# Conversions of w_in beside attention on GpSimd, four early loads, and shared low parts of w_out

## The chip, the cores and the metric

The kernel runs on one core of one Trainium2 chip. The metric is device time of one execution in microseconds (us); lower is better. The engines are TensorE (PE in the rows, its weight loads PEld), VectorE (DVE), ScalarE (ACT), GpSimd (POOL) and SyncE (SP), which here only issues transfers. A name with a q behind it (SPq, POOLq) is an engine's queue of instructions that are not computation, such as transfers.

## The reference

Three parts follow one another. The inputs are float32 but for w_in and w_out, which are float64; the kernel reads these two as 64-bit words.

```python
# attention: q, k, v [4, 12, 448, 64]
scores = cap * np.tanh((q @ k.T / 8) / cap)
attn = softmax(scores)                     # sum + 1e-9
x = (attn @ v) -> [1792, 768]
# top-1 mixture of 8 experts, 768 -> 1024 -> 768
e = argmax(x @ w_gate); gate = softmax(x @ w_gate)[e]
x = gate * (relu(x @ w1[e]) @ w2[e])
# MLP, 768 -> 2048 -> 768
h = x @ w_in
g = (a0 + a1*h + a2*h**2 + a3*h**3) / (1 + |b0|*|h| + |b1|*h**2 + 1e-6)
out = g @ w_out
```

## The kernel before

One program runs the three parts. Within it the order in which each engine gets its instructions is the order in which the code issues them (`manual_schedule`), so where a line stands in the code decides what it waits behind. Each engine takes its instructions strictly in that order.

**Attention** runs over 24 pairs of heads (`attention`, n = 0 to 23; a batch is 6 pairs). A pair's scores go through tanh and exp on ScalarE in four chunks (L143 to L151), VectorE adds the chunks (`presum`, L157, two per pair, tile `ts`), and TensorE makes the products with v (L166, L168) and the sums S (L178). In the loop's order the sums of pair n-1 come in pair n, behind `presum(n - 1, 1)`. Two batches' gates and rows are worked in between. `between(n)` is called twice per pair with `more`, and each such call steps the generator `conv_in` once.

**Conversion of w_in** (`conv_in`) takes 48 such steps, three for each of 16 tiles n. A tile arrives as 128 x 1536 32-bit words (`ci_raw`, two buffers), the two halves of 768 float64 numbers. ScalarE makes the exponent part from the upper words (`conv_a0`, L1090, tile `ci_a`, one buffer) in step one, and the lower words' part (`conv_a1`, L1093, tile `ci_hl`) in step two. In step three VectorE shifts and merges (`conv_b`, L1096 and L1097), SP issues the load of tile n+2, and GpSimd adds (`conv_c`, L1100), rounds to the high part (`pcopy`, L259) and subtracts for the low part (L1145). SP stores the pair of parts to `wi` in the next tile's step two.

**The experts** run after the gate in slots of 128 tokens (`phase_b`, about 300 to 613 us), and convert w_out in the same manner beside them. Their weights' buffers are `w1h` and `w1l`, four each; at the end the MLP's rings are laid into these and other buffers that are free by then (`mlp_start`).

**The MLP** (`phase_c`, `blocks`) has 5 blocks of 3, 3, 3, 3 and 2 tiles of 128 tokens, with 16 steps (n) of 128 hidden units each. Step n does `first(n)` (18 matmuls with x and w_in, each a product of high and low parts, L1336 to L1338), `rational(n)` (five activations on ScalarE, L1348 to L1352, beginning with the Square; three operations on GpSimd, L1353 to L1355; reciprocal, product and low part of the result on VectorE, L1356 to L1362, with its rounding on ScalarE, L1361), and `second` for two earlier steps (L1371 to L1373): half nh = 0 of w_out with step n - 4 (`LAG`), half nh = 1 with step n - 16. The last 16 steps of the loop (n from 80) have no `first`: they are called the drain here, and the results are sent by GpSimd from the rows' order (L1382, L1383).

w_in's parts come back through `win_load` on GpSimd's queue (L1304) into a ring of four; loads 0 and 1 are issued in `mlp_start`, 2 and 3 in `phase_c`, and load n + 3 in step n. Parts of w_out come by SP as single float32 tiles and are split in place: `wout_high` rounds on ScalarE (L1316), `wout_low` subtracts (L1322), on VectorE for nh = 0 and on GpSimd for nh = 1. In the trace the buffers keep the names of their first use, so that `w1h` and `w1l`, `raw`, `ex` and `x` stand in the MLP for parts of these rings.

Of the kernel before, what the change touches and what calls it, by code (L numbers as in the profile page):

```python
# [8 lines left out]
F32 = mybir.dt.float32  # L9
F32R = mybir.dt.float32r  # L10
BF16 = mybir.dt.bfloat16
U32 = mybir.dt.uint32
I32 = mybir.dt.int32
AF = mybir.ActivationFunctionType
ALU = mybir.AluOpType
# [7 lines left out]
DM = H * D  # L23
# [17 lines left out]
class K:  # L41
# [1072 lines left out]
    def conv_in(self, pool):  # L1114

        w = self.i["w64"].bitcast(U32)
        raws = {}

        def load(n):
            if n < self.NF:  # L1120
                raws[n] = pool.tile([128, 2 * DM], U32, name=f"ci_raw{n}", tag="ci_raw", bufs=2)
                self.nc.sync.dma_start(out=raws[n], in_=w[n])

        def store(n):
            if n in done:
                self.nc.sync.dma_start(out=self.wi[n], in_=done.pop(n).bitcast(F32))

        done = {}
        load(0)
        load(1)  # L1130
        for n in range(self.NF):
            a = pool.tile([128, DM], U32, name=f"ci_a{n}", tag="ci_a", bufs=1)
            hl = pool.tile([128, 2 * DM], F32R, name=f"ci_hl{n}", tag="ci_hl", bufs=2)
            raw = raws.pop(n).rearrange("p (c w) -> p c w", w=2)
            r = hl[:, DM:].bitcast(U32)
            self.conv_a0(a, raw)
            yield
            self.conv_a1(r, raw)
            store(n - 1)
            yield  # L1140
            self.conv_b(a, raw)
            load(n + 2)
            self.conv_c(a, r)
            self.pcopy(hl[:, :DM], r.bitcast(F32))
            self.nc.gpsimd.tensor_tensor(out=hl[:, DM:], in0=r.bitcast(F32), in1=hl[:, :DM].bitcast(F32), op=ALU.subtract)  # L1145
            done[n] = hl
            yield
        store(self.NF - 1)
# [85 lines left out]
    def mlp_start(self):  # L1234
        raw = self.raw[0] + self.raw[1]
        h, l = self.w1
        W = 384
        cut = lambda tiles: self.ring(tiles, W)[1]
        self.rings = {"win": [-1, [h[2], l[2]]]}
        c = cut([h[3], l[3]])  # L1240
        wout = [(c[2 * k], c[2 * k + 1]) for k in range(4)]
        self.rings |= {"wos0": [0, wout[:2]], "wos1": [0, wout[2:]]}
        a, b, c, d = (cut([t]) for t in raw[1:5])
        self.rings |= {"wor0": [0, c[:3]], "wor1": [0, d[:3]], "u": [0, [*a[2:], b[0]]], "o": [0, [*b[1:], c[3], d[3], *cut(self.xg[:1])]]}
        c = cut(raw[5:8])
        self.rings |= {k: [0, c[3 * i : 3 * i + 3]] for i, k in enumerate("stpq")}
        for f in range(2):
            self.win_load(f)
        for f in range(3):
            self.wout_load(0, f)  # L1250
        xt = self.p_xt.rearrange("p a b -> p (a b)")
        self.rings["ph"] = [0, self.p_l1]
        self.rings["xt"] = [0, [self.p_ht[0], xt[:, :512]]]
        self.acc = [[xt[:, :512], xt[:, 512:], self.p_ht[0]], [self.p_ht[1], *self.p_l2]]
        h, l = (cut(t[:2]) for t in (h, l))
        self.x2 = [[h[:6], l[:6]], [h[6:], l[6:]]]

    def phase_c(self):
        W = 384
        with self.tc.tile_pool(name="mlp", bufs=1) as mp:  # L1260
            xh, xl = (self.ring([t.rearrange("p a b -> p (a b)")], W)[1] for t in (self.xh, self.xl))
            for k in range(2):
                self.rings[f"wos{k}"][1].append((xh[k], xl[k]))
            self.rings["win"][1] += [mp.tile([128, 2 * DM], F32R, name=f"win{k}") for k in range(2)]
            self.win_load(2)
            self.win_load(3)
            for t, nm in zip(self.x2[1], "hl"):
                t += [mp.tile([128, W], F32R, name=f"x2{nm}{k}") for k in range(2, 6)]
            self.gh, self.gl = ([mp.tile([128, W], F32R, name=f"g{p}{f}") for f in range(self.NF)] for p in "hl")
            self.blocks()  # L1270
# [48 lines left out]
    def wout_low(self, nh, n):  # L1319
        if 0 <= n < len(self.BLOCKS) * self.NF:  # L1320
            h, l, r = self.wout[nh, n]
            (self.nc.gpsimd if nh else self.nc.vector).tensor_tensor(out=l, in0=r, in1=h.bitcast(F32), op=ALU.subtract)  # L1322
            self.wout_load(nh, n + 3)

    def first(self, n, kcs=range(6), ph=None):
# [154 lines left out]
```

## Time and profile before

| | |
|---|---|
| time, median of 3 runs | 1146.98 us (1144.69 to 1149.13) |
| profiled execution | 1150.3 us; span 1148.7 us; mean granted clock 0.975 |
| PE busy, share of the span | 1059.4 us (92%) |
| DVE, ACT, POOL busy | 698.1 (61%), 695.4 (61%), 650.9 us (57%) |
| memory | 247.12 MB moved, mean 215 GB/s |

The span is the part of the execution between its first and last instruction in the profile. A row of a timeline gives the start, the time it took, the engine, line and operation, the tile written and read, and in square brackets the engine's idle time ahead of it and what ended that. The granted clock is TensorE's, 1.0 for its upper level of 2.4 GHz; a stretch at 0.5 runs at the lower, 1.2 GHz.

### The profile page before, as it was taken

Reading aid. Unit: us, or ns where it says so; the run is one execution under the profiler, and the core shown is the slowest. Engines: PE = TensorE matmul, PEld = TensorE weight load, DVE = VectorE, ACT = ScalarE, POOL = GpSimd, SP = SyncE. Lnnn points to the kernel's source line nnn. Section 1 sums busy time; section 2 is a strip of 40 time slices with the busy share of each in tenths; the row PEclk is TensorE's granted clock in tenths of the full one; section 3 lists DMA queues with packets and bytes.
Section 4 is the critical chain, followed back from the end, with each engine's and each line's share of the span. In section 5 each row is a group of like instructions: output and inputs, shape, how many; then the busy total and the mean of one; then the engine's idle time right before and its main releaser. Section 6 shows DMA issues by size and latency. Waiting matters only on the chain. (4 is left out here: it accounts for less than half of the span.)

```text
span 1148.7 us, 17160 instructions
## 1 busy us (share of the span) xinstructions
PE 1059.4 (92%) x5808; PEld 857.9 (75%) x5808; DVE 698.1 (61%) x857; ACT 695.4 (61%) x1084; POOL 650.9 (57%) x631
## 2 busy tenths in 40 slices
PE   6999999895899989998999689999999999999985
PEld 2232322234798888988988678999999999999984
DVE  2557575768839463856373677766666666665660
ACT  5978788672347452835362566666666666676552
POOL 2433333356426443554332656786788688779975
PEclk9999999997999999998999899999999999999998
DMA  6696968745598775797514556665677576657843
GB/s 168 210 268 191 265 203 249 231 174 193 191 361 323 275 264 202 279 327 261 205 61 148 198 171 194 221 207 184 200 234 220 174 223 210 205 185 235 252 147 96
DMA packets 96439, 247.12 MB, mean 215 GB/s; under 512 B 12320, under 2 KB 61376, under 8 KB 96320
## 3 DMA queue, kind: packets, MB, share of 16 engines
q1 hardware_dynamic: 78624, 161.22, 43.0%
q0 software_dynamic: 17248, 82.62, 22.4%
q10 hardware_dynamic: 448, 1.80, 0.4%
q8 instruction: 60, 0.98, 0.3%
q14 instruction: 59, 0.48, 0.1%
HBM read 202.93 MB, written 42.67 MB: 214 GB/s over the span
## 5 line engine op out<-in xcount | busy, mean ns | idle before, releaser
L1356 DVE RECIPROCAL raw<-raw 128x384 f32<-128x384 f32 (+1 forms) x80 | 191.3, 2392 | 163.0 <-POOL raw L1354 163.0
L834 PE MATMUL p_l<-w1h,x 128*128 128x512 f32 x432 | 144.0, 400 | 1.4 <-ACT x L798 1.4
L1353 POOL TENSOR_TENSOR ex<-ex 128x384 f32<-128x384 f32 (+1 forms) x80 | 79.3, 991 | 98.8 <-ACT ex L1350 98.1
L1348 ACT ACTIVATE ex<-p_l 128x384 f32<-128x384 f32 (+1 forms) x80 | 37.7, 471 | 145.7 <-PE p_l L1338 141.1
L1100 POOL TENSOR_TENSOR ci_hl<-ci_hl,ci_a 128x768 int32<-128x768 int32 x16 | 37.2, 2327 | 149.5 <-ACT ex L151 36.4
L855 PE MATMUL p_l<-w2h,hh 128*128 128x384 f32 x288 | 102.3, 355 | 10.2 <-issue 7.2
L136 PE MATMUL sc<-qq,kk 64*128 64x448 f32 (+1 forms) x384 | 96.5, 594 | 10.2 <-ACT ex L143 5.1
L857 PE MATMUL p_l<-w2h,hl 128*128 128x384 f32 x288 | 99.1, 344 | 2.3 <-DVE hl L800 2.3
L856 PE MATMUL p_l<-w2l,hh 128*128 128x384 f32 x288 | 98.8, 343 | 1.5 <-issue 1.5
L834 PEld LDWEIGHTS p_l<-w1h,x 128*128 128x128 f32 x432 | 82.0, 190 | 18.5 <-ACT x L798 2.2
L800 DVE TENSOR_TENSOR hl<-p_ht,hh 128x512 fp32r<-128x512 f32 x36 | 24.8, 690 | 106.3 <-ACT hh L798 106.1
L834 PE MATMUL p_l<-w1l,x 128*128 128x512 f32 x216 | 85.2, 396 | 0.9 <-POOL w1l L800 0.9
L1354 POOL TENSOR_TENSOR raw<-raw,ex 128x384 f32<-128x384 f32 (+1 forms) x80 | 79.8, 998 | 8.4 <-ACT raw L1352 1.2
L143 ACT ACTIVATE ex<-sc,icap 128x896 f32<-128x896 f32 x72 | 71.1, 1004 | 21.8 <-PE sc L136 21.4
L837 ACT ACTIVATE hr<-p_l 128x512 f32<-128x512 f32 x36 | 21.6, 599 | 103.2 <-PE p_l L834 103.2
L151 ACT ACTIVATE ex<-ex,cap 128x1792 f32<-128x1792 f32 (+1 forms) x48 | 76.9, 1603 | 1.0
L136 PEld LDWEIGHTS sc<-qq,kk 64*128 64x128 f32 (+1 forms) x384 | 29.9, 178 | 63.2 <-issue 32.9
L867 POOL DMA_DIRECT2D x2d<-y x36 | 20.5, 569 | 96.5 <-DVE y L860 63.5
L166 PE MATMUL av<-ex,vv 128*64 128x448 f32 x288 | 68.3, 562 | 4.0 <-ACT ex L151 4.0
L1336 PE MATMUL p_l<-w1h,win 128*128 128x384 f32 (+1 forms) x176 | 58.7, 334 | 11.3 <-DMA win<-wi 6.3
L1100 POOL TENSOR_TENSOR c_r<-c_r,c_a 128x768 int32<-128x768 int32 x20 | 36.9, 1845 | 49.2 <-ACT c_a L1090 34.3
L855 PEld LDWEIGHTS p_l<-w2h,hh 128*128 128x128 f32 x288 | 55.7, 193 | 11.3 <-issue 10.0
(341 smaller groups left out, 3302.6 us busy)
## 6 DMA issues: line engine op xcount, KB each, us to landing
win<-wi POOLq DMA_DIRECT2D x40, 768.0 KB, 4.6
raw<-in_w SPq DMA_DIRECT2D x34, 768.0 KB
ex<-in_w SPq DMA_DIRECT2D x32, 768.0 KB
raw<-wd SPq DMA_DIRECT2D x80, 192.0 KB
w1h<-wi POOLq DMA_DIRECT2D x20, 768.0 KB, 4.7
w1l<-wi POOLq DMA_DIRECT2D x20, 768.0 KB, 6.2
ex<-wd SPq DMA_DIRECT2D x80, 192.0 KB
ci_raw<-in_w SPq DMA_DIRECT2D x16, 768.0 KB
```

The lines of the kernel that those rows point to most:

```text
L136: nc.tensor.matmul(o, kk[half[a], 128 * c : min(128 * c + 128, S)], qq[half[a]], start=True, stop=True)
L143: nc.scalar.activation(out=es[n][:, 2 * c : 2 * c + 2], in_=pt[:, :, :S], func=AF.Tanh, scale=self.icap)
L151: nc.scalar.activation(out=e, in_=e, func=AF.Exp, scale=self.cap)
L166: nc.tensor.matmul(at[half[a], :S], vv[:, a, c], e[:, 2 * c + a], start=c == 0, stop=False, skip_group_check=True)
L834: nc.tensor.matmul(pt, a[:, kc, :], b, start=kc == 0 and k == 0, stop=kc == 5 and k == 2)
L855: nc.tensor.matmul(pt[:, :384], hh, wh, start=f == 0, stop=False)
L856: nc.tensor.matmul(pt[:, :384], hh, wl, start=False, stop=False)
L857: nc.tensor.matmul(pt[:, :384], hl, wh, start=False, stop=f == 7)
L1100: self.nc.gpsimd.tensor_tensor(out=r.bitcast(I32), in0=r.bitcast(I32), in1=a.bitcast(I32), op=ALU.add)
L1353: nc.gpsimd.tensor_tensor(out=q, in0=q, in1=s, op=ALU.mult)
L1354: nc.gpsimd.tensor_tensor(out=u, in0=u, in1=t, op=ALU.add)
L1356: nc.vector.reciprocal(out=u, in_=u)
```

## The change

It has three parts. In `conv_in` the two activations become `tensor_scalar` operations on GpSimd, in the first of a tile's three steps, together with the store of the tile before; `conv_b` and the load of tile n+2 come in the second and the rest in the third; `ci_a` has two buffers. In `mlp_start` the ring of `win` is laid into the last expert's four weight buffers and all four loads are issued there, and the ring for w_out's split gets new tiles in their place. In `wout_low` the engine depends on the step: for nh = 0 odd steps below 12 go to GpSimd, and for nh = 1 even steps from 66 on go to VectorE.

```diff
--- before.py
+++ after.py
@@ -1128,21 +1128,22 @@
         done = {}
         load(0)
         load(1)
+        P = self.nc.gpsimd
         for n in range(self.NF):
-            a = pool.tile([128, DM], U32, name=f"ci_a{n}", tag="ci_a", bufs=1)
+            a = pool.tile([128, DM], U32, name=f"ci_a{n}", tag="ci_a", bufs=2)
             hl = pool.tile([128, 2 * DM], F32R, name=f"ci_hl{n}", tag="ci_hl", bufs=2)
             raw = raws.pop(n).rearrange("p (c w) -> p c w", w=2)
             r = hl[:, DM:].bitcast(U32)
-            self.conv_a0(a, raw)
-            yield
-            self.conv_a1(r, raw)
+            P.tensor_scalar(out=a.bitcast(F32), in0=raw[:, :, 1].bitcast(F32), scalar1=2.0**-112, scalar2=0.0, op0=ALU.mult, op1=ALU.add)
+            P.tensor_scalar(out=r.bitcast(I32), in0=raw[:, :, 0], scalar1=2.0**-29, scalar2=0.0, op0=ALU.mult, op1=ALU.add)
             store(n - 1)
             yield
             self.conv_b(a, raw)
             load(n + 2)
+            yield
             self.conv_c(a, r)
             self.pcopy(hl[:, :DM], r.bitcast(F32))
-            self.nc.gpsimd.tensor_tensor(out=hl[:, DM:], in0=r.bitcast(F32), in1=hl[:, :DM].bitcast(F32), op=ALU.subtract)
+            P.tensor_tensor(out=hl[:, DM:], in0=r.bitcast(F32), in1=hl[:, :DM].bitcast(F32), op=ALU.subtract)
             done[n] = hl
             yield
         store(self.NF - 1)
@@ -1236,15 +1237,12 @@
         h, l = self.w1
         W = 384
         cut = lambda tiles: self.ring(tiles, W)[1]
-        self.rings = {"win": [-1, [h[2], l[2]]]}
-        c = cut([h[3], l[3]])
-        wout = [(c[2 * k], c[2 * k + 1]) for k in range(4)]
-        self.rings |= {"wos0": [0, wout[:2]], "wos1": [0, wout[2:]]}
+        self.rings = {"win": [-1, [h[2], l[2], h[3], l[3]]]}
         a, b, c, d = (cut([t]) for t in raw[1:5])
         self.rings |= {"wor0": [0, c[:3]], "wor1": [0, d[:3]], "u": [0, [*a[2:], b[0]]], "o": [0, [*b[1:], c[3], d[3], *cut(self.xg[:1])]]}
         c = cut(raw[5:8])
         self.rings |= {k: [0, c[3 * i : 3 * i + 3]] for i, k in enumerate("stpq")}
-        for f in range(2):
+        for f in range(4):
             self.win_load(f)
         for f in range(3):
             self.wout_load(0, f)
@@ -1260,10 +1258,8 @@
         with self.tc.tile_pool(name="mlp", bufs=1) as mp:
             xh, xl = (self.ring([t.rearrange("p a b -> p (a b)")], W)[1] for t in (self.xh, self.xl))
             for k in range(2):
-                self.rings[f"wos{k}"][1].append((xh[k], xl[k]))
-            self.rings["win"][1] += [mp.tile([128, 2 * DM], F32R, name=f"win{k}") for k in range(2)]
-            self.win_load(2)
-            self.win_load(3)
+                new = [tuple(mp.tile([128, W], F32R, name=f"wo{p}{k}{i}") for p in "hl") for i in range(2)]
+                self.rings[f"wos{k}"] = [0, [(xh[k], xl[k]), *new]]
             for t, nm in zip(self.x2[1], "hl"):
                 t += [mp.tile([128, W], F32R, name=f"x2{nm}{k}") for k in range(2, 6)]
             self.gh, self.gl = ([mp.tile([128, W], F32R, name=f"g{p}{f}") for f in range(self.NF)] for p in "hl")
@@ -1319,7 +1315,9 @@
     def wout_low(self, nh, n):
         if 0 <= n < len(self.BLOCKS) * self.NF:
             h, l, r = self.wout[nh, n]
-            (self.nc.gpsimd if nh else self.nc.vector).tensor_tensor(out=l, in0=r, in1=h.bitcast(F32), op=ALU.subtract)
+
+            eng = n % 2 if not nh and n < self.NF - self.LAG or nh and n >= (len(self.BLOCKS) - 1) * self.NF + 2 else nh
+            (self.nc.gpsimd if eng else self.nc.vector).tensor_tensor(out=l, in0=r, in1=h.bitcast(F32), op=ALU.subtract)
             self.wout_load(nh, n + 3)
 
     def first(self, n, kcs=range(6), ph=None):
```

The conversion of tile 0 in VectorE's order, in attention's second pair (`ex_127` are the exponentials of pair 0, `av` the products, `u` their copy). Before:

```order
L157 TENSOR_TENSOR ts_207<-ex_127 128x896
L157 TENSOR_TENSOR ts_207<-ts_207,ex_127 128x896
L182 COPY u_241<-av_209 128x448
L1096 TENSOR_SCALAR ci_a_200<-ci_a_200 128x768
L1097 SCALAR_TENSOR_TENSOR ci_a_200<-ci_raw_196,ci_a_200 128x768
L157 TENSOR_TENSOR ts_259<-ex_128 128x896
```

and now:

```order
L157 TENSOR_TENSOR ts_208<-ex_127 128x896
L1096 TENSOR_SCALAR ci_a_200<-ci_a_200 128x768
L1097 SCALAR_TENSOR_TENSOR ci_a_200<-ci_raw_196,ci_a_200 128x768
L157 TENSOR_TENSOR ts_208<-ts_208,ex_127 128x896
L182 COPY u_245<-av_210 128x448
```

The two rows of `conv_b` moved ahead of pair 0's second presum.

GpSimd's order at the end of the experts and the start of the MLP (`x2d` are the experts' results, `wi` the parts of w_in, the three TENSOR_TENSOR rows `rational`). Before:

```order
L1304 DMA w1h_1907<-wi 128x1536
L1304 DMA w1l_1910<-wi 128x1536
...
L1353 TENSOR_TENSOR ex_128<-ex_128 128x384
L1354 TENSOR_TENSOR raw_130<-raw_130,ex_127 128x384
L1355 TENSOR_TENSOR ex_127<-ex_127,ex_128 128x384
L1304 DMA win_9268<-wi 128x1536
L1304 DMA win_9269<-wi 128x1536
L1304 DMA w1h_1907<-wi 128x1536
```

and now (the lines moved up by four):

```order
L1300 DMA w1h_1907<-wi 128x1536
L1300 DMA w1l_1910<-wi 128x1536
L1300 DMA w1h_1968<-wi 128x1536
L1300 DMA w1l_1969<-wi 128x1536
...
L1351 TENSOR_TENSOR ex_128<-ex_128 128x384
L1352 TENSOR_TENSOR raw_130<-raw_130,ex_127 128x384
L1353 TENSOR_TENSOR ex_127<-ex_127,ex_128 128x384
L1300 DMA w1h_1907<-wi 128x1536
```

Two loads moved from behind the first `rational` to right behind the first two.

VectorE's last instructions, in the drain (`wol`, `x` and `w1h` are w_out's low parts). Before:

```order
L1358 TENSOR_TENSOR ex_127<-ex_128,raw_131 128x256
L1322 TENSOR_TENSOR w1h_1968<-raw_132,w1h_1968 128x384
L1362 TENSOR_TENSOR gl_9311<-ex_127,gh_9295 128x256
L1322 TENSOR_TENSOR w1h_1968<-raw_132,w1h_1968 128x384
L1322 TENSOR_TENSOR x_1904<-raw_132,x_1903 128x384
L1377 COPY raw_131<-p_l_2042 128x384
```

and now:

```order
L1356 TENSOR_TENSOR ex_127<-ex_128,raw_131 128x256
L1320 TENSOR_TENSOR x_1904<-raw_132,x_1903 128x384
L1360 TENSOR_TENSOR gl_9317<-ex_127,gh_9301 128x256
L1320 TENSOR_TENSOR wol_9271<-raw_132,woh_9270 128x384
L1320 TENSOR_TENSOR wol_9275<-ex_127,woh_9274 128x384
L1320 TENSOR_TENSOR wol_9273<-raw_132,woh_9272 128x384
L1320 TENSOR_TENSOR x_1904<-ex_127,x_1903 128x384
L1320 TENSOR_TENSOR wol_9277<-ex_127,woh_9276 128x384
L1320 TENSOR_TENSOR wol_9275<-ex_127,woh_9274 128x384
L1320 TENSOR_TENSOR x_1904<-ex_127,x_1903 128x384
L1320 TENSOR_TENSOR wol_9277<-ex_127,woh_9276 128x384
L1320 TENSOR_TENSOR wol_9275<-ex_127,woh_9274 128x384
```

Seven subtractions from `ex_127`, half nh = 1, came over from GpSimd.

## Rows read from the trace of the kernel before

**Rows 1.** Stretches: start:end, length, busy us (count) per engine, clock, DMA share, GB/s

```profile
0.00:30.00 30.00, 18.90 (x70) 6.58 (x70) 6.96 (x23) 15.78 (x16) 8.42 (x18) 0.94 0.66 177
30.00:90.00 60.00, 57.71 (x289) 17.10 (x290) 34.78 (x47) 50.92 (x51) 23.10 (x13) 1.00 0.79 231
632.00:670.00 38.00, 26.09 (x119) 25.14 (x118) 28.22 (x22) 19.03 (x38) 22.60 (x25) 0.82 0.59 198
800.00:1100.00 300.00, 296.67 (x1800) 295.69 (x1799) 197.33 (x214) 197.18 (x428) 241.08 (x283) 1.00 0.68 213
1114.00:1118.00 4.00, 3.84 (x13) 3.84 (x14) 1.47 (x4) 1.08 (x4) 3.53 (x4) 0.57 0.46 139
```

**Rows 2.** ACT's timeline, start of attention

```profile
17.01 0.89 ACT L1090 ACTIVATE ci_a<-ci_raw 128x768 f32<-128x768 f32 x1 [5.03 <-DMA ci_raw<-in_w]
```

**Rows 3.** PE's timeline, attention

```profile
18.85 3.43 PE L136 MATMUL sc<-qq,kk 64*128 64x448 f32 x8 [5.10 <-ACT ex L143]
...
24.03 0.57 PE L178 MATMUL S<-ts,sel 128*32 128x448 f32 x2
...
31.23 0.97 PE L166 MATMUL av<-ex,vv 128*64 128x448 f32 x4 [1.04 <-ACT ex L151]
...
89.70 0.57 PE L178 MATMUL S<-ts,sel 128*32 128x448 f32 x2 [0.62 <-DVE ts L157]
```

**Rows 4.** Source line L1090: duration min/median/max in ns, and what ended idle time

```profile
L1090 ACT ACTIVATE ci_a<-ci_raw x16: 879/916/940, 17.0 to 235.9; 128x768 f32<-128x768 f32 x16
...
  POOL ci_hl L1100: 5.7, 4
```

**Rows 5.** POOL's timeline, start of the MLP

```profile
633.81 1.13 POOL L1304 DMA_DIRECT2D win<-wi  x2
```

**Rows 6.** The page's DMA issues: count, KB each, median us to landing

```profile
win<-wi POOLq DMA_DIRECT2D x40, 768.0 KB, 4.6
```

**Rows 7.** PE's timeline, start of the MLP

```profile
638.51 0.66 PE L1336 MATMUL p_l<-w1h,win 128*128 128x384 f32 x1 [6.27 <-DMA win<-wi]
...
664.46 0.69 PE L1336 MATMUL p_l<-w1h,win 128*128 128x384 f32 x1 [2.41 <-DVE w1l L800]
```

**Rows 8.** PE's timeline, drain

```profile
1114.16 0.44 PE L1372 MATMUL p_xt<-w1h,gh 128*128 128x384 f32 x1 [1.85 <-DVE w1h L1322]
```

**Rows 9.** Waits, 1096 to 1149 us: total, times, longest

```profile
PE p_ht L1372 <- POOL w1l L1322: 3.0, 4, 1.1
```

**Rows 10.** Source line L259 (`pcopy`), as in rows 4

```profile
L259 POOL TENSOR_SCALAR ci_hl<-ci_hl x16: 830/834/1552, 29.0 to 250.4; 128x768 fp32r<-128x768 f32 x16
```

**Rows 11.** POOL's timeline, attention's second batch

```profile
93.48 1.82 POOL L1100 TENSOR_TENSOR ci_hl<-ci_hl,ci_a 128x768 int32<-128x768 int32 x1 [5.77 <-ACT ex L145]
```

**Rows 12.** DVE's timeline, attention

```profile
21.44 1.09 DVE L157 TENSOR_TENSOR ts<-ts,ex 128x896 f32<-128x896 f32 x1 [8.34 <-ACT ex L151]
...
24.69 0.55 DVE L1096 TENSOR_SCALAR ci_a<-ci_a 128x768 uint32<-128x768 uint32 x1
25.27 0.96 DVE L1097 SCALAR_TENSOR_TENSOR ci_a<-ci_raw,ci_a 128x768 uint32<-128x768 uint32 x1
...
94.19 1.14 DVE L518 TENSOR_SCALAR ji<-ri 112x4 int32<-112x4 int32 x1
95.36 0.16 DVE L520 TENSOR_TENSOR jt<-ri,ji 112x4 f32<-112x4 int32 x1
```

**Rows 13.** SP's queue, start

```profile
12.80 0.47 SPq L122 DMA_DIRECT2D kk<-in_k  x1
```

**Rows 14.** ACT's timeline, start of the MLP (Square of steps 1 and 2)

```profile
632.28 0.49 ACT L1348 ACTIVATE ex<-p_l 128x384 f32<-128x384 f32 x1 [0.44 <-PE p_l L1338]
...
644.21 0.49 ACT L1348 ACTIVATE ex<-p_l 128x384 f32<-128x384 f32 x1 [6.30 <-PE p_l L1338]
```

**Rows 15.** DVE's timeline, start of the MLP

```profile
658.43 1.37 DVE L1322 TENSOR_TENSOR x<-raw,x 128x384 fp32r<-128x384 f32 x1
```

**Rows 16.** POOL's timeline, drain

```profile
1127.71 1.00 POOL L1322 TENSOR_TENSOR w1l<-ex,w1l 128x384 fp32r<-128x384 f32 x1
```

## The prediction

> **What bounds the kernel now.** I read the table of stretches first, to see where an engine is full. From 800 to 1100 us, inside the MLP's blocks, TensorE is busy 296.67 of 300 us, and at attention's full pace, 30 to 90 us, 57.71 of 60 [rows 1]: in both only the last per cents can be won. Three stretches are thinner: the first 30 us with 18.90 busy; the head of the MLP, 632 to 670 us, with 26.09 of 38 us at a mean granted clock of 0.82; and the drain, where after a pause 13 matmuls take 3.84 us at a clock of 0.57, against 1800 in 300 us, 0.167 each, in the full blocks [rows 1]. So the change is priced in four places, and the timelines of the engines tell what TensorE waits for in each.
>
> In the start, ScalarE stands 5.03 us until 17.01 for the first raw tile, because the conversion L1090 is in its queue; TensorE's scores follow at 18.85 after 5.10 us of nothing, and the sums S at 24.03 [rows 2, 3]. Later ScalarE waits 4 times, 5.7 us in all, for GpSimd's L1100 to free the one buffer `ci_a` [rows 4]; behind the first of these TensorE loses 1.04 at 31.23, behind the second 0.62 before the sums at 89.70 [rows 3].
>
> In the MLP head TensorE waits 6.27 us for `win`, until 638.51: the load went out on GpSimd at 633.81 only, and one takes 4.6 us to land [rows 5 to 7]. In the drain it waits for the subtractions of w_out's split: 1.85 us for VectorE's at 1114.16, then 3.0 us in four waits for GpSimd's [rows 8, 9].
>
> **Part 1, conversions on GpSimd.** Off ScalarE go 32 activations at about 0.91, 29 us: the 16 of L1090 by their median of 0.916, the 16 of L1093 taken alike [rows 4]. GpSimd gets 32 operations with one tensor input of 128x768. The trace of before has none of just this form. The nearest is `pcopy`, the same engine, operation and size with another stride and output type: median 0.834 [rows 10]. The upper end is 1.82, L1100 with two inputs [rows 11], the lower `pcopy`'s shortest, 0.83. I take 0.85, close to `pcopy`: 27 us, at the upper end 58. GpSimd is busy 23.10 of 60 us there [rows 1], so there is room for it.
>
> Start: ScalarE no longer stands at 11.98. But VectorE now has `conv_b` of tile 0 ahead of the second presum, and that needs the raw tile (17.01) and one GpSimd operation (0.85). It runs from about 17.9 for 0.55 + 0.96, then the presum for 1.1, to 20.5, where it ended at 22.5 before [rows 12]. The sums, which then wait for nothing else, would start near 20.6, 3.4 us before 24.03. TensorE idles longer ahead of them and may lose clock, so I take **2.5**, ends 1 and 5. The wait at 31.23 goes: **1.0**. The three like it at a batch's start lie between 0.62 and 1.04; 0.8 each: **2.4**.
>
> Against this stands VectorE. While GpSimd's L1100 ran from 93.48 to 95.30, the tiny `ji` took 1.14 and ended with it; `jt`, right after, took 0.16 [rows 11, 12]. So a VectorE operation can be held for the rest of a GpSimd operation, up to 0.85 for each of 32 new ones, 27 us in all. Most of it is hidden, since VectorE works 34.78 of 60 us [rows 1] and TensorE asks for its result later; I count 0.4 in sum. Attention: 2.5 + 1.0 + 2.4 - 0.4 = **5.5**, ends -2 and 10.
>
> The Trainium skill has a rule that speaks against this part ("SBUF — State Buffer", section "Who interferes with whom"): VectorE and GpSimd share one port pair, which whoever issues first holds alone for its whole instruction, while ScalarE has ports of its own. The trace agrees with it (1.14 against 0.16). Taken at its word for every overlap it gives the fourth rival; with most holds hidden it leaves the sum as it is.
>
> On SP the load of raw tile 2 now stands ahead of pair 3's q, k and v and waits for `conv_b` of tile 0. They went out at 12.80 [rows 13] and will go at about 20; pair 3's scores come behind 31.23, so 10 us remain, and nothing is lost. The stores of `wi` move one step; they are read after 613 us.
>
> **Part 2, four loads at once, w_out's low parts of block 0 shared.** Loads 2 and 3 move from behind rational(0), at 633.81, to right behind loads 0 and 1, at about 616. If the four landed strictly one after the other at 4.6 us [rows 6], the third would be there at about 616 + 3 x 4.6 = 630 and the fourth at 634.5. first(2) can start at 638.51 - 6.27 = 632.24 [rows 7], and first(3) needs its own 18 matmuls of 0.167 later [rows 1], at 635.2. Covered; the pause goes, and the half clock behind it.
>
> What is late next is the chain behind it. ScalarE's Square of step 2 started at 644.21 after 6.30 of waiting [rows 14]; it can start when `gh` of step 0 and the high split before it are through, at about 637.9: 6.3 gained. From there on VectorE and GpSimd set the pace. VectorE's low part of step 1, 1.37, stood ahead of a reciprocal [rows 15]; it is now GpSimd's, at 1.00 [rows 16]. TensorE's next pause, 2.41 until 664.46 [rows 7], shrinks, and the slow matmuls behind it, worth about 1. GpSimd was busy 22.60 of 38 us [rows 1] and its rational can stand up to 1.0 behind a new low part; I take 1.2 back in all. 6.3 + 1.4 + 1.0 - 1.2 = **7.5**. The lower end is 3, if VectorE and GpSimd hold each other as they did the 1.37; the upper 10, both pauses and the 1.37. The blocks behind run at TensorE's pace and pass the shift on whole.
>
> **Part 3, drain.** Of the 1.85 at 1114.16 I take half, 0.9: VectorE's low part there stands behind its own reciprocal and product, and half of the parts change engine. The 13 slow matmuls cost 3.84 - 13 x 0.167 = 1.7 over full speed [rows 1]; after the shorter pause at 31.23 the products ran at full pace [rows 3], so I count 1.0 of it. Then GpSimd did each low part in 1.00 between sends [rows 16] while VectorE was idle; sharing takes 2 of the 3.0 us of waits [rows 9]. 3.9, so **4**; ends 1 (the transfers of w_out bind instead) and 6.5 (all of it).
>
> **Sum.** 5.5 + 7.5 + 4 = 17. The profiled execution took 1150.3 (span 1148.7), so 1133.3 by its count; it lies 3.3 over the median of the runs shown, 1146.98, and from that the forecast is **1130.0**. A measurement of this kernel can tell about 0.5%, 5.7 us, from no change.
>
> **Rivals.**
> 1. *Attention gives nothing.* Holds of VectorE and the wait for the first raw tile, only moved to VectorE, eat the 5.5. For it: `ji` at 1.14. Against: TensorE's waits on ScalarE are seen and their cause is removed. 11.5 gained: 1135.5.
> 2. *The head trades one wait for another.* VectorE, 28.22 of 38 us busy [rows 1], keeps the pace; 3 of 7.5, so 12.5 gained: 1134.5.
> 3. *All at its upper values.* ScalarE was the fuller helper in attention, 50.92 of 60 us [rows 1]; without 29 us of conversions most pauses close, 10, with 9 in the head and 6 in the drain: 1122.
> 4. *Slower.* The new operations cost 1.82 like two-input ones [rows 11] and hold VectorE's presums, on which TensorE's sums wait: 58 us of holds, half of them reaching TensorE, 29, less the 11.5 of the other parts and the 4.4 of ScalarE's waits: 1160. It decides from 16 us of reached holds on, 9 of 32 at 1.82 or 19 at 0.85. Against it: GpSimd already works 23.10 of 60 us there, most of it two-input, and TensorE idles 2.3 [rows 1].
> 5. *The early loads don't act.* They collide with the last expert's transfers and land no sooner than needed: the head gives 0: 1137.5. The bound of one after the other speaks against it.
>
> **Chances.** Forecast 0.55, the rivals in turn 0.14, 0.10, 0.12, 0.05, 0.04. The forecast's own spread, from the ends of its terms, is about 7 to either side. The range is **1118 to 1142**: it holds the forecast and the single rivals but the fourth, and leaves out the sum of several lower ends, and of all upper ends. Faster by over 0.5% (under 1141.2) is all but the fourth rival and the worst of the first, second and fifth together, 0.89; within 0.5% 0.06; slower 0.05.
>
> **What would show it.** Right: no wait of ScalarE for the raw tile and the first sums at 20 to 22; the moved operations at 0.8 to 0.95 on GpSimd; first(2) right behind first(1) and step 2's Square 6 us sooner against it; a granted clock over 0.9 in the head; in the drain low parts on both engines in turn, and less than 1.5 us of waits for GpSimd's. Wrong: moved operations over 1.3 us; TensorE's waits for VectorE in attention growing by more than those for ScalarE shrink; a `win` wait still ahead of first(2), or its Square less than 4 us sooner.

## The result and the profile after

The changed kernel takes 1126.80 us (median of 4 runs, 1125.03 to 1128.83), the kernel before, run beside it, 1146.35. The ratio is 0.9828, interval 0.9800 to 0.9855: 19.6 us less. The forecast was 1130.0, 17 us less than before, with a range of 1118 to 1142.

The profiled execution of the change took 1125.84 us (span 1124.0), 24.5 less than that of before. It is more than the medians differ. From the first to the last relu of the experts, code that the change doesn't touch, the profiled executions of all the kernels below spread from 348.5 to 352.8 us; before took 352.4 there and the change 349.7. So 2.7 of the 24.5 lie in a stage that varies by as much on its own. Another 1.4 lie between the Squares of steps 16 and 79 of the MLP, where each execution takes either about 379.9 or about 381.4, whichever parts of the change it has. Stages are therefore compared below over several runs.

The table of stretches of the changed kernel, at the places of [rows 1] (head and drain moved with the program):

```profile
0.00:30.00 30.00, 21.66 (x78) 6.77 (x78) 10.20 (x24) 16.70 (x16) 14.77 (x22) 0.94 0.77 211
30.00:90.00 60.00, 59.68 (x302) 17.87 (x302) 37.24 (x52) 45.21 (x43) 33.19 (x21) 1.00 0.77 235
622.34:660.34 38.00, 30.17 (x162) 28.84 (x161) 31.86 (x26) 25.58 (x51) 30.80 (x32) 0.96 0.60 187
790.00:1090.00 300.00, 297.98 (x1818) 297.29 (x1818) 192.56 (x217) 201.34 (x440) 242.22 (x286) 1.00 0.67 212
1092.00:1096.00 4.00, 3.38 (x19) 3.39 (x20) 3.77 (x7) 1.75 (x4) 3.61 (x4) 1.00 0.48 150
```

TensorE's share rose where it was thin: the head from 26.09 to 30.17 us of 38, at a clock of 0.96 for 0.82; the drain's start now does 19 matmuls in 4 us at full clock, 13 before. The 60 us of attention went from 57.71 to 59.68, and the full blocks are as they were. What TensorE still waits for, in its timeline:

```profile
20.80 0.57 PE L178 MATMUL S<-ts,sel 128*32 128x448 f32 x2 [3.00 <-DVE ts L157]
...
96.09 0.57 PE L178 MATMUL S<-ts,sel 128*32 128x448 f32 x2 [1.78 <-DVE ts L157]
...
214.91 0.57 PE L178 MATMUL S<-ts,sel 128*32 128x448 f32 x2 [2.94 <-DVE ts L157]
...
631.16 0.44 PE L1334 MATMUL p_l<-w1h,w1h 128*128 128x384 f32 x1 [2.33 <-ACT ex L1349]
...
638.78 0.44 PE L1370 MATMUL p_xt<-wol,gh 128*128 128x384 f32 x1 [4.04 <-DVE wol L1320]
...
1092.62 0.44 PE L1370 MATMUL p_xt<-x,gh 128*128 128x384 f32 x1 [1.06 <-DVE x L1320]
```

The sums of pair 0 start at 20.80 (24.03 in [rows 3]), behind a new wait of 3.00 for VectorE. Behind that wait TensorE is slow for a while: from 22 to 25 us its granted clock is 0.51 in the change and 0.95 in before, as the two windows show, the change first:

```profile
22.00:25.00 3.00, 3.00 (x10) 0.46 (x8) 1.37 (x1) 1.06 (x2) 2.83 (x3) 0.51 1.02 309
```

```profile
22.00:25.00 3.00, 3.00 (x18) 0.65 (x16) 1.39 (x3) 2.96 (x3) 0.00 (x0) 0.95 0.00 0
```

The 5.10 before the scores of [rows 3] and the 6.27 for `win` of [rows 7] are gone; the 1.85 of [rows 8] is 1.06. The moved operations by source line, and `pcopy` beside them:

```profile
L1137 POOL TENSOR_SCALAR ci_a<-ci_raw x16: 875/912/1807, 16.7 to 228.1; 128x768 f32<-128x768 f32 x16
...
L259 POOL TENSOR_SCALAR ci_hl<-ci_hl x16: 832/1552/1823, 22.5 to 238.6; 128x768 fp32r<-128x768 f32 x16
```

The moved operations take 0.91 in the median, as the activations did [rows 4], but `pcopy`, 0.834 in [rows 10], now takes 1.55.

From the timelines I read five numbers for each kernel: ScalarE's first copy of the sums (L264, "start"), the three distances from one batch's first such copy to the next batch's (the third holds pair 20), the Square of step 16 of the MLP less that of step 1 ("head"), and the last matmul's end less the Square of step 79 ("drain").

| kernel | start | three batches | head | drain |
|---|---|---|---|---|
| before | 49.83 | 58.78, 58.80, 63.93 | 93.87 | 32.29 |
| the change | 47.09 | 59.50, 57.91, 59.90 | 84.18 | 28.39 |
| e1, conversion alone | 48.93 | 59.50, 57.90, 59.89 | 91.69 | 32.50 |
| e2, loads alone | 50.52 | 58.78, 58.79, 64.59 | 85.96 | 32.30 |
| e3, low parts of block 1 alone | 50.64 | 58.78, 58.79, 63.90 | 91.09 | 30.70 |
| e4, drain alone | 50.55 | 58.79, 58.78, 63.91 | 92.98 | 27.63 |
| e5, change on ScalarE | 50.37 | 57.78, 57.79, 59.18 | 84.16 | 28.52 |
| e6, change, merge late | 42.38 | 60.53, 60.43, 66.28 | 84.15 | 28.28 |
| e7, change, doubled operations | 49.55 | 57.90, 57.90, 63.27 | 84.11 | 27.98 |
| e8, change, tile 0 late | 42.80 | 57.90, 57.89, 59.89 | 84.67 | 27.85 |
| e9, e8 with ScalarE | 42.43 | 57.78, 57.79, 59.18 | 84.07 | 27.81 |
| e10, before, second buffer | 49.25 | 58.41, 58.40, 63.73 | 93.02 | 32.48 |
| e11, e5 with one buffer | 48.77 | 57.79, 57.78, 59.18 | 84.20 | 27.60 |
| e12, e8 with an early low part | 43.56 | 57.89, 57.91, 61.28 | 85.46 | 27.80 |

Each row is one execution. Start, head and drain scatter by 1 to 2 us for the same code. The batches repeat to 0.1 with three exceptions, all of the clock: the 59.50 of the change and e1 against the 57.90 of e7, e8 and e12, the 61.28 of e12 against e8's 59.89, and e2's 64.59 (its granted clock is 0.54 from 223 to 226 us, 0.72 from 222 to 225 in before). The same pause of TensorE, 1.78 before the sums, is followed by a lower granted clock in the change and by a full one in e8, as windows on the two show, the change first:

```profile
95.00:100.00 5.00, 3.91 (x14) 0.82 (x14) 4.83 (x10) 1.57 (x2) 1.72 (x2) 0.72 0.58 210
```

```profile
90.00:95.00 5.00, 3.22 (x20) 0.89 (x20) 4.86 (x10) 2.52 (x3) 2.43 (x2) 1.00 0.59 210
95.00:100.00 5.00, 5.00 (x27) 1.48 (x26) 2.62 (x4) 2.71 (x3) 4.08 (x3) 1.00 0.65 197
```

The clock's fall there costs 1.6 us, and whether it comes differs between executions.

### The profile page after: what moved, and what is told of

Its sections match the earlier page's. It is cut to its first block, busy times and chain, and to the rows that moved or that the text cites. A ratio compares the mean times of both kernels' runs of the same rounds, so it can differ in the third digit from the quotient of the medians.

```text
span 1124.0 us, 17161 instructions
## 1 busy us (share of the span) xinstructions
PE 1053.4 (94%) x5808; PEld 851.6 (76%) x5808; DVE 698.7 (62%) x858; ACT 671.9 (60%) x1052; POOL 690.2 (61%) x662
## 5 line engine op out<-in xcount | busy, mean ns | idle before, releaser
L136 PE MATMUL sc<-qq,kk 64*128 64x448 f32 (+1 forms) x384 | 98.0, 603 | 5.2 <-DMA kk<-in_k 5.2
L1100 POOL TENSOR_TENSOR ci_hl<-ci_hl,ci_a 128x768 int32<-128x768 int32 x16 | 32.5, 2033 | 88.3 <-DVE ci_a L1097 68.6
L136 PEld LDWEIGHTS sc<-qq,kk 64*128 64x128 f32 (+1 forms) x384 | 29.6, 178 | 58.2 <-issue 40.0
L1100 POOL TENSOR_TENSOR c_r<-c_r,c_a 128x768 int32<-128x768 int32 x20 | 36.9, 1845 | 48.0 <-ACT c_a L1090 32.4
L1334 PE MATMUL p_l<-w1h,w1h 128*128 128x384 f32 (+1 forms) x176 | 57.0, 324 | 6.1 <-DVE x2l L800 2.6
```

What stands on the lines that cost most here:

```text
L136: nc.tensor.matmul(o, kk[half[a], 128 * c : min(128 * c + 128, S)], qq[half[a]], start=True, stop=True)
L1100: self.nc.gpsimd.tensor_tensor(out=r.bitcast(I32), in0=r.bitcast(I32), in1=a.bitcast(I32), op=ALU.add)
```

## The experiments

### The four parts alone (e1 to e4)

e1 is the kernel before with the diff of `conv_in` alone, e2 with that of `mlp_start` and `phase_c`, e3 and e4 with one half of the rule in `wout_low`:

```diff
 # e3
+            eng = n % 2 if not nh and n < self.NF - self.LAG else nh
 # e4
+            eng = n % 2 if nh and n >= (len(self.BLOCKS) - 1) * self.NF + 2 else nh
```

> Only the conversion beside attention is changed (GpSimd, new order of its three steps, two buffers of ci_a). If its saving is local and stays, the copy of the first sums (L264) comes 2.7 us sooner than before's 49.83 and the first matmul of the experts near 245 instead of 251.95; the time falls by 5.5 to 7 us, ratio near 0.994 to 0.995. If the trace of the whole change only happened to show 7 us there, or the experts' stage gives it back, it falls by under 3 us.

Measured: 1141.35 us, ratio 0.9934 (0.9910 to 0.9959), 7 us less, as expected of a saving that stays. The first copy, at 48.93, is only 0.9 sooner and not 2.7: TensorE waits 3.59 ahead of the first sums, 3.00 in the change, and its granted clock is still 0.60 from 25 to 28 us (0.92 in the change). Attention ends 5.1 us sooner (last copy 245.55 for 250.67).

> Only the four early loads of w_in with the new rings. If the missing load was the wait that counted, the Square of step 2 comes 5.5 us closer to that of step 1 (6.4 instead of 11.9 us behind it) and the step of 16 about 7 to 9 us sooner against step 1; ratio near 0.993. If VectorE and GpSimd take the wait over without the shared low parts, step 16 gains under 4 us: ratio near 0.997.

Measured: 1141.70, ratio 0.9940 (0.9918 to 0.9963). Step 2's Square is 6.41 behind that of step 1 (11.93 before), and the head takes 85.96: 6 to 8 less than in the kernels with the old loads and the old low parts (91.7 to 93.9). The first theory holds.

> Only the odd low parts of nh = 0 of the first twelve steps go to GpSimd. If VectorE's queue is a limit of the first block by itself, step 16 comes 1 to 3 us sooner against step 1. If the late load sets the pace, or GpSimd is as full as VectorE, nothing is gained, or up to 1.5 us lost; the total within 0.3% of before either way.

Measured: 1146.36, ratio 0.9986 (0.9970 to 1.0002). The head takes 91.09, which lies at the edge of the scatter (91.7 to 93.9 without the part). The step from e2's 85.96 to the 84.1 to 84.2 that most kernels with both edits show is the better reading, 1.8 us, though it rests on one execution of e2.

> Only the sharing of nh = 1 from step 66 on. If GpSimd's low parts were the limit of the drain, the time from the Square of step 79 to the last matmul falls from 32.1 us by 3.5 to 5.5 us and TensorE no longer drops to its lower clock there; ratio near 0.996. If the transfers of w_out are the limit, it falls by under 1.5 us.

Measured: 1143.56, ratio 0.9958 (0.9942 to 0.9975). The drain takes 27.63 instead of 32.29; the clock stays up at its start, where in before it is 0.57 [rows 1]:

```profile
1107.00:1111.00 4.00, 2.94 (x18) 2.62 (x17) 4.00 (x7) 2.58 (x7) 3.70 (x5) 1.00 0.27 87
```

The four ratios less one add up to -1.82%, against -1.72% for the whole. So no part is seen to hide another; by the intervals, one that hid less than about 0.5%, 5 us, would not show.

### Order or engine in attention (e5, e6, e10, e11)

The table shows that in the change the first two batches gave -0.7 (with the clock's fall; 0.9 without it, as in e8) and 0.9, and the third 4.0, where the prediction had 2.4 for all and nothing for pair 20. The timelines of the kernel before at pair 20, GpSimd's and VectorE's, say what the third batch had lost. Beside pair 20 VectorE works the third batch's gate and finds the expert that will run first (`favourite`, from L563 on), a chain of small operations:

```profile
214.48 1.81 POOL L1100 TENSOR_TENSOR ci_hl<-ci_hl,ci_a 128x768 int32<-128x768 int32 x1 [9.17 <-issue]
216.37 0.84 POOL L259 TENSOR_SCALAR ci_hl<-ci_hl 128x768 fp32r<-128x768 f32 x1
217.29 1.82 POOL L1145 TENSOR_TENSOR ci_hl<-ci_hl 128x768 fp32r<-128x768 f32 x1
```

```profile
210.06 0.17 DVE L563 TENSOR_REDUCE favmx<-rk 128x1 f32<-128x8 f32 x1 [1.83 <-PE rk L505]
...
212.80 0.55 DVE L1096 TENSOR_SCALAR ci_a<-ci_a 128x768 uint32<-128x768 uint32 x1
213.38 0.96 DVE L1097 SCALAR_TENSOR_TENSOR ci_a<-ci_raw,ci_a 128x768 uint32<-128x768 uint32 x1
...
214.45 1.86 DVE L571 TENSOR_SCALAR fav<-iom,favmx 128x8 f32<-128x8 f32 x1
...
217.35 1.78 DVE L584 TENSOR_SCALAR nf<-fav 8x8 f32<-8x8 f32 x1
...
219.12 1.07 DVE L157 TENSOR_TENSOR ts<-ts,ex 128x896 f32<-128x896 f32 x1
```

and TensorE's:

```profile
220.25 0.96 PE L178 MATMUL S<-ts,sel 128*32 128x448 f32 x2 [4.17 <-DVE ts L157]
```

Two operations on 8 columns are held for as long as L1100 and L1145 run, the merge (L1096, L1097) stands in the same row, the presum comes behind them all, and TensorE idles 4.17 us and comes back at a lower clock (0.96 for 0.57 us). In the change the merge of this tile comes half a pair sooner, and GpSimd does the tile from 205.72 on. So order and engine had to be told apart. e5 puts ScalarE back; e6 puts the merge, with the load behind it, back into the third step:

```diff
 # e5
-            P.tensor_scalar(out=a.bitcast(F32), ...
-            P.tensor_scalar(out=r.bitcast(I32), ...
+            self.conv_a0(a, raw)
+            self.conv_a1(r, raw)
 # e6
             store(n - 1)
             yield
+            yield
             self.conv_b(a, raw)
             load(n + 2)
-            yield
             self.conv_c(a, r)
```

> The whole change, but the two conversions of w_in stay on ScalarE; the new order of the steps and the two buffers are kept. If the 4 us won in attention's last batch came from the order (the shift-and-merge half a pair sooner, so that GpSimd's two-input operations no longer run beside pair 20's gate), that batch still takes 59 to 61 us from the copy of sums ahead of it to its own, and only the start is lost: first copy of the sums at 49 to 51 instead of 47.1, total 2 to 4 us over the change. If it came from the engine, the last batch takes 63 to 65 again and the total is 6 to 8 us over the change.

Measured: 1126.55, ratio 0.9831 (0.9788 to 0.9873), the same as the change. The third batch takes 59.18: the order makes it. The total isn't 2 to 4 us longer as expected, as far as an interval of 0.85% can tell (one of the four runs took 1136.33). The start is 3.3 us later (50.37), but the batches are shorter than the change's by 1.7, 0.1 and 0.7 (1.6 of it the clock's fall), and attention ends within 0.7 us of the change (244.44 and 243.73).

> The whole change, but VectorE's shift-and-merge and the load behind it stand in the third step again; the conversions stay on GpSimd. If the order makes the gain at pair 20, the last batch takes 63 to 65 us as in the kernel before, while the first sums no longer wait behind the merge of tile 0: first copy at 44.5 to 46.5. Total 1 to 3 us over the change. If the engine makes it, the last batch stays at 60 and the total is 1 to 3 us under the change.

Measured: 1134.31, ratio 0.9871 (0.9847 to 0.9894), 5 us over the change by the ratio, where 1 to 3 were expected; in the traces attention ends 5.2 later (248.94 for 243.73). The start comes sooner than I expected (42.38), and the batches are longer than before's, all three (60.5, 60.4, 66.3). TensorE's row at pair 20 is that of before:

```profile
217.15 0.96 PE L178 MATMUL S<-ts,sel 128*32 128x448 f32 x2 [4.17 <-DVE ts L157]
```

With the merge late, GpSimd's new operations cost 1.6 us or more a batch, clock included (TensorE pauses 1.99 before a sum at 83.25); with the new order ScalarE is as good a place for them.

What the order does at pair 20 can be read from the chain. VectorE's and GpSimd's timelines of the change there:

```profile
205.95 0.17 DVE L563 TENSOR_REDUCE favmx<-rk 128x1 f32<-128x8 f32 x1 [0.38 <-PE rk L505]
...
208.93 1.77 DVE L567 TENSOR_TENSOR fav<-fav,iota 128x8 f32<-128x8 f32 x1
...
213.77 1.08 DVE L157 TENSOR_TENSOR ts<-ts,ex 128x896 f32<-128x896 f32 x1
```

```profile
205.72 1.81 POOL L1100 TENSOR_TENSOR ci_hl<-ci_hl,ci_a 128x768 int32<-128x768 int32 x1 [6.69 <-DVE ci_a L1097]
...
208.56 2.12 POOL L1146 TENSOR_TENSOR ci_hl<-ci_hl 128x768 fp32r<-128x768 f32 x1
210.64 1.81 POOL L1137 TENSOR_SCALAR ci_a<-ci_raw 128x768 f32<-128x768 f32 x1
```

From L563 to the presum the chain takes 9.06 us in before and in e6, 8.45 in e7, 7.82 in the change and 6.87 in e5 and e11. TensorE's wait behind it is 4.17, 3.55, 2.94 and 1.99: it follows the chain to 0.02. So GpSimd's two-input operations have not left the chain, against the expectation of e5: they run beside it in the change too, and L567 is now held for 1.77. Added up, the holds of the chain are 0.2 us longer than before. What left it is the merge itself, 1.46 us from 212.80 to 214.26. Without the moved operations beside it (e5) the chain is 0.95 shorter still.

The order comes with a second buffer of `ci_a`. e10 is before with `bufs=2`, e11 is e5 with `bufs=1`.

> The kernel before with one edit: ci_a has two buffers. If the 1.4 us waits of ScalarE for that buffer are what the steady batches lose, the first two batches take 57.8 us instead of 58.8 and the last stays at 63 to 65; total 2 to 3 us under before. If the order is needed for it, batches stay at 58.8 and the total within 1 us of before.

Measured: 1147.40, ratio 0.9990 (0.9968 to 1.0012), the same as before. Batches are 0.4 shorter, less than the 1.0 of the first case, and TensorE's wait at pair 20 is 4.17, as it was.

> The whole change with the conversions on ScalarE, the new order, and one buffer of ci_a. If order makes the gain at pair 20 and the buffer that of the other batches, the batches take about 58.8, 58.8 and 59 to 61 us; total 1 to 3 us over the change. If the buffer is needed for both, the last takes 63 to 65 again: 5 to 7 us over the change.

Measured: 1127.11, ratio 0.9829 (0.9793 to 0.9865). Neither of my two cases: all batches are those of e5, with one buffer. The wait of [rows 4] is gone all the same, as the view by source line of ScalarE's conversion shows; the add of a tile is now through before the next tile's conversion comes:

```profile
L1090 ACT ACTIVATE ci_a<-ci_raw x16: 887/911/926, 16.1 to 228.1; 128x768 f32<-128x768 f32 x16
...
its engine sat idle before it (us, times) until:
  DMA ci_raw<-in_w: 3.7, 1
```

So with ScalarE's conversions and the new order the second buffer does nothing, and the order alone makes what attention gains from pair 2 on. No run has GpSimd's conversions with one buffer.

### What GpSimd's operations cost (e7)

```diff
+            P.tensor_scalar(out=a.bitcast(F32), ...   # each of the two lines a second time
```

> The whole change, with each of the two conversions issued twice on GpSimd (the same result twice): 32 more operations of 0.9 us, 29 us. If VectorE's waits for the shared port are mostly hidden beside TensorE's work, the time rises by under 4 us, 1 of them at the first sums. If such waits reach TensorE, as in the forecast's slower case, it rises by 10 us or more.

Measured: 1130.37, ratio 0.9846 (0.9822 to 0.9870); by the ratios 2 us over the change, with intervals that overlap. In the traces attention ends 4.2 later (247.94 for 243.73): 2.5 at the start, 3.4 in the third batch, where TensorE again waits and comes back slow, and 1.6 less in the first, where the clock stayed up.

```profile
216.40 0.96 PE L178 MATMUL S<-ts,sel 128*32 128x448 f32 x2 [3.55 <-DVE ts L157]
```

29 us more on GpSimd cost 6 in two places, the start (where 1 to 2 can be scatter) and pair 20's gate, and nothing in the two other batches. The forecast's slower case is refuted in size: it needed 16.

### Further versions (e8, e9, e12)

TensorE's 3.00 ahead of the first sums are the price of the merge of tile 0 in front of the presum. e8 gives `between` the number of calls, leaves out the one in pair 0's first half and makes two in pair 1's second, so that only tile 0 moves; the cut shows the two calls:

```diff
-            between(n)
+            between(n, 0 if n == 0 else 1)
 ...
-            between(n)
+            between(n, 2 if n == 1 else 1)
```

> The whole change, with tile 0's first two steps of the conversion one call later and its third beside tile 1's first, so that the merge of tile 0 stands behind the first sums; from pair 2 on the order is that of the change. If TensorE's 3.0 us ahead of the first sums are due to the merge alone, the first sums start at 17.5 to 18.5 instead of 20.8, the first copy comes 2.5 to 3.5 us sooner, and the total falls 2 to 3.5 us under the change: ratio to before about 0.980. If the raw tile's transfer or ScalarE then holds the next pair as long, it falls by under 1 us.

Measured: 1124.56, ratio 0.9798 (0.9777 to 0.9820): 3 us under the change by the ratios, though the intervals overlap. The first sums start at 17.64 without a wait, the first copy comes 4.3 us sooner than in the change, and the last 5.9 (1.6 of it the clock's fall in the change):

```profile
17.64 0.57 PE L178 MATMUL S<-ts,sel 128*32 128x448 f32 x2
```

e9 is e8 with tiles 1 to 15 converted on ScalarE, so that each engine does what costs least there.

> The change with tile 0's merge behind the first sums (as in the run before it), tile 0 converted on GpSimd and the 15 others on ScalarE. If the order is the gain and GpSimd's operations only a cost after tile 0, the first copy of the sums stays near 42.8 and the batches take 57.8, 57.8 and 59.2 us instead of 57.9, 57.9 and 59.9: attention's last copy 0.5 to 1.5 us before 237.8, total 0 to 2 us under that run. If GpSimd relieves ScalarE in earnest, it comes 2 us or more later.

Measured: 1123.45, ratio 0.9783 (0.9755 to 0.9811). The batches are those expected, and the last copy comes at 236.51 for e8's 237.81. The total is the same as e8's within the intervals. No run has this order with tile 0 on ScalarE too, so whether GpSimd is needed at all stays open.

e12 is e8 with the first low part of w_out ahead of the third reciprocal; behind it, where it stood, it is left out (not in the cut):

```diff
                 self.wout_high(nh, second[nh] + 2)
+            if n == 2:
+                self.wout_low(0, 0)
```

> The change with tile 0's merge behind the first sums, and in the MLP the first low part of w_out (step 0, nh = 0) issued on VectorE ahead of the third reciprocal, where VectorE was idle 0.9 us, instead of behind it. If that low part's place is what TensorE's 4.0 us ahead of the first second-half matmuls hang on, that wait falls under 1.5 us; the step of 16 comes 1 to 2.5 us sooner against step 1 (84.2 to 84.7 there), total 1 to 2 us less. If the chain of reciprocals alone sets the first block's pace, the wait falls but step 16 gains under 0.7.

Measured: 1123.12, ratio 0.9778 (0.9751 to 0.9804), not to be told from e8 and e9. The wait of 4.03 for the low part is gone, but the next first half-step waits 4.27 in its place, and the step of 16 comes 0.8 later against step 1 (85.46 for 84.67). That is what the second theory said, that the chain through the reciprocals sets block 1's pace. TensorE now waits for ScalarE, and ScalarE, ahead of that, for the product behind VectorE's reciprocal:

```profile
640.07 0.69 PE L1334 MATMUL p_l<-w1h,w1l 128*128 128x384 f32 x1 [4.27 <-ACT ex L1349]
```

```profile
637.10 0.51 ACT L1359 CAST gh<-ex 128x384 fp32r<-128x384 f32 x1 [1.92 <-DVE ex L1356]
```

No run shortens the reciprocals, so the chain's part is read from these rows and not tested by itself.

## Why the prediction was right, and where it was not

**The sum.** 17 was forecast, 19.6 measured. By stages, with the kernels of the table that have a part against those that haven't: attention about 6.7 (forecast 5.5; the means of the last copy, 251.4 in before and e2 to e4, 244.6 in the change and e1), head about 8.7 (7.5; 92.9 and 84.2), drain about 4.1 (4; 32.1 and 28.0).

**Attention: about right in its sum, wrong in its terms.** Between the profiled executions of before and the change attention gave 6.9. Two forecast terms lie ahead of the first copy of the sums, the start's 2.5 and the 1.0 of the wait at 31.23; together they gave 2.7 in the change and 0.9 in e1. The merge was at 17.62 and the sums at 20.80, as worked out (17.9 and 20.6), 3.2 sooner than in before. But the half clock behind the new wait, shown at the top, took back half of it: two groups of matmuls later the scores (L136) start at 26.78 for 28.42. So the start gave 1.6 and not 2.5; the risk had been named, and priced too low. The wait at 31.23 is gone and gave the other 1.1. The moved operations take 0.91 where I took 0.85. The three steady waits, "0.8 each: 2.4", were sized about right, 0.9 or 1.0 a batch (58.8 to 57.9 or 57.8), less a fall of the clock of 1.6 in the first batch that I had not counted.

The step that failed is a missing term: pair 20, to which I gave nothing. The third batch gave 4.0. Its steady wait, 1.06 in before, with small ones beside it, accounts for 1.2 of this, pair 20 for 2.8: the chain is 1.2 shorter, and TensorE, which came out of its 4.17 us of waiting at a lower clock in before and out of 2.94 at full clock in the change, runs the same matmuls, from the sums to those of L614, in 1.6 less. I had counted how the new operations hold VectorE, and not what it means that the old ones move: the merge left the gate's chain. The clock's 1.6 is not sure to come: in e12, with the same order, it fell there, and the third batch took 61.28. That the sum came out near the forecast is in part luck: the start's shortfall and the clock's fall in the first batch, 2.4 together, were made up by pair 20.

The reason given for the steady term was wrong, too. I put it to ScalarE's relief by GpSimd; with the conversions on ScalarE the waits are gone as well and the time is the same (e5, e11). What GpSimd itself brings is the first copy of the sums, 1.7 to 3.3 us sooner; it costs 0.9 in the three batches (57.90, 57.89, 59.89 against 57.78, 57.79, 59.18) and 1.6 more where the clock falls. The order does the rest.

**The holds.** They are real: in e5 and e11 TensorE waits 1.99 at pair 20, in the change 2.94, where two of the moved operations (L1137 at 210.64 and L1138 behind it, until 213.44) now stand beside the gate. That 0.9 is twice the forecast's 0.4. By the Trainium skill's rule on the shared port ("SBUF — State Buffer", "Who interferes with whom") VectorE and GpSimd can hold each other. The traces agree, both ways: `pcopy` at 1.55 instead of 0.83, and 8-column operations at 1.8. But a hold alone gives no time: e7 shows that 29 us more of such work cost 4.

**Head.** Loads: forecast 6.3 and about 1 from the second pause; measured 6 to 8. The mechanism held step by step; the second pause, 2.41 at 664.46, is 1.17 in the change. first(2) follows first(1) without a pause, and its Square comes 6.4 behind that of step 1 where it was 11.9 [rows 14]; in ScalarE's timeline of the change:

```profile
622.62 0.49 ACT L1346 ACTIVATE ex<-p_l 128x384 f32<-128x384 f32 x1 [0.44 <-PE p_l L1336]
...
628.20 0.51 ACT L1359 CAST gh<-ex 128x384 fp32r<-128x384 f32 x1 [2.90 <-DVE ex L1356]
...
629.03 0.48 ACT L1346 ACTIVATE ex<-p_l 128x384 f32<-128x384 f32 x1
```

That is 5.5 for the 6.3 forecast: `gh` of step 0 comes 5.58 behind the first of these rows, 0.9 more than before, since the product it waits for is now held longer beside GpSimd's operations and takes 2.12 (1.26 before). The next wait was the low part's, 4.04 us; before had 3.23 there, which the prediction did not price. e12 showed that with it gone TensorE waits as long for the next step. The shared low parts were worth 1.8 (1.4 had been the forecast, with 1.2 given back).

**Drain.** 4 forecast, 4.1 measured, with the terms about as forecast: the 1.85 became 1.06, the clock stayed up (1.00 for 0.57), and the waits for GpSimd's low parts fell from 3.0 to half:

```profile
PE p_ht L1370 <- POOL wol L1320: 1.5, 3, 0.6
```

**The rivals.** The first (attention gives nothing) and the third (all at upper values) didn't come; the second fell with e2, the fifth with the absence of a wait for `win`. The fourth is refuted by e1 and e7. Its sum took 4.4 for ScalarE's waits where the forecast's own terms add up to 5.9 (2.5, 1.0 and 2.4); with these it would have been 1158.6, and the answer is the same.

## What to carry to other kernels

When a change moves an operation to another engine and also to another place in the order, price the two apart, and run them apart: in attention the engine was worth nothing that the total shows (e5 against the change), and the merge's place about 5 us (e6 against it). Where a third engine waits on a chain of small operations, add up everything that stands in that chain on its own engine, and what the neighbour holds of it: here the wait followed the chain's length to 0.02 us, and taking the merge of 1.46 us out of it was worth more than taking away the operations beside it, 0.95. A second buffer is only worth its memory if the wait for the first is still there once the order is right.

## What the runs showed of the hardware that was not expected

Holds go both ways. GpSimd's 128x768 `pcopy` took 0.83 where VectorE did nothing large and 1.55 beside VectorE's presums, which themselves took 2.16 (1.08 alone) behind a GpSimd operation, as VectorE's and GpSimd's timelines of the change show at the start:

```profile
21.20 2.16 DVE L157 TENSOR_TENSOR ts<-ex 128x896 f32<-128x896 f32 x1
```

```profile
19.90 2.52 POOL L1100 TENSOR_TENSOR ci_hl<-ci_hl,ci_a 128x768 int32<-128x768 int32 x1 [0.96 <-DVE ci_a L1097]
22.50 1.55 POOL L259 TENSOR_SCALAR ci_hl<-ci_hl 128x768 fp32r<-128x768 f32 x1
```

L1100 ends at 22.42, the presum 0.94 later at 23.36, near its 1.08 alone; `pcopy` ends at 24.05, 0.69 after that, near its 0.83. So here the two engines ran these operations one after the other.

After the same pause TensorE's clock fell in one execution and not in another. After 1.77 or 1.78 us before the sums it fell in the change and e1 and stayed up in e7, e8 and e12. After 2.93 or 2.94 it stayed up in the change, e1 and e8 (sums at 0.57) and fell in e12 (0.96). After 4.17 and 3.55 at pair 20 it fell in every run, with the first sums or right behind them. At 1.4 to 1.6 us a time this can be a part of the scatter between executions, and it is over half of what pair 20 gave.
